# K of an attention decode loaded in 8 KB rows, with successive rows alternating between the partition halves

## The chip, the cores and the metric

The kernel runs on one core of a Trainium2 chip. Inputs lie in HBM; 16 DMA engines copy them to SBUF, where the tensors of this kernel have up to 128 partitions (rows). SP is the engine that issues these loads here; TensorE multiplies matrices, into PSUM; VectorE and ScalarE work on elements. A packet is one entry of the trace's record of DMA transfers. The metric is the device time of one execution in microseconds (us). Eight executions of the kernel before took 196.13 to 197.31 us, seven of them 196.13 to 196.50. Ratios are the mean time of one kernel's fast runs over that of the other's of the same rounds, so they are not quite the ratios of the medians quoted beside them. A single look ("one run") carries no state; it is used only for differences far larger than the scatter.

## The reference

One decode step of attention with a sliding window: 32 batches, 32 query heads, 8 key/value heads, head size 128, and the last 512 of 2048 cached positions.

```
q = (x @ wq)                                  # x: 32 x 512, wq: 512 x 4096
k, v = k_cache[:, :, -512:, :], v_cache[:, :, -512:, :]   # 32 x 8 x 512 x 128, bf16
p = softmax(q . k * 128**-0.5)                # four query heads share a key head
out = (p . v) @ wo                            # wo: 4096 x 512
```

K and V are read once, 33.6 MB each; wq and wo add 8.4 MB. For each of the 32 batches the core needs 1 MB of K and 1 MB of V. The inputs are so small that the softmax is nearly uniform. "Correct" below therefore says little about K.

## The kernel before

SP issues all loads. A batch of K is two loads of 512 KB (four heads each), a batch of V likewise. Each load fills 128 partitions with one row of 4 KB: partition 4s+g holds 16 consecutive positions (chunk s of 32) of head g.

```
NS = 32; NR = 16
K_sb = sb("K_sb", [P, NK, 2, NR, DH], BF16)

def cache_rows(cache, b, h):
    return cache[b, 4*h:4*h+4, SK-W:, :].rearrange("g (s r) d -> s g (r d)", s=NS)

def load_k(b):
    if b >= NK:
        sp.wait_ge(pe_T[3], b - NK + 1)
    for h in range(2):
        sp.dma_start(K_sb[:, b % NK, h].rearrange("p r d -> p (r d)"),
                     cache_rows(k_cache, b, h)).then_inc(sem_k[b % NK][h], 16)
...                                   # load_v: the same with V_sb and sem_v
for b in range(B + LEAD):             # LEAD = 5: K runs five batches ahead of V
    if b < B: load_k(b)
    if b >= LEAD: load_v(b - LEAD)
```

TensorE transposes K (32 products per batch), VectorE and ScalarE copy the result to KT_sb, TensorE makes the scores of four batches in S_ps, in PSUM, and then come softmax, another transpose, and the products with V. The constant `perm` orders the columns of the transposed K, so the placing of rows on partitions can be chosen freely.

Of the kernel before, what the change touches and what calls it, by code (L numbers as in the profile page):

```python
# [1 line left out]

# [3 lines left out]
BF16 = mybir.dt.bfloat16  # L6
F32 = mybir.dt.float32
ACTF = mybir.ActivationFunctionType
ALU = mybir.AluOpType
# [3 lines left out]
def bass_standalone__sliding_block_cached__sampling_kernel(  # L13
# [16 lines left out]
    G4 = 4  # L30
    NR = 16
    NS = 32
    DKT = D // 128
    SCALE = float(DH) ** -0.5
    P = 128
# [11 lines left out]
    with ExitStack() as es:  # L47
# [4 lines left out]
        w_sb = sb("w_sb", [P, DKT * HD], BF16)  # L52
        wq_sb = w_sb[:, :].rearrange("p (kt n) -> p kt n", kt=DKT)
        wo_sb = w_sb[:, :].rearrange("p (g i n) -> p g i n", g=NHG, i=4)
        K_sb = sb("K_sb", [P, NK, 2, NR, DH], BF16)
        V_sb = sb("V_sb", [P, NV, 2, NR, DH], BF16)
        KT_sb = sb("KT_sb", [P, NKT, 2, NR, G4, NS], BF16)
        QT_sb = sb("QT_sb", [P, HQ, B], BF16)
        QBD = sb("QBD", [P, NQB, G, 32], BF16)
        P_f32 = sb("P_f32", [P, W], F32)  # L60
# [4 lines left out]
        band = sb("band", [P, 4, 224], BF16)  # L65
        xT_sb = sb("xT_sb", [P, DKT, 32], BF16)
        ident = sb("ident", [P, P], BF16)
        perm = sb("perm", [P, G4, NS], BF16)
        x_sb = sb("x_sb", [32, D], BF16)
        out_sb = sb("out_sb", [32, 4, 128], BF16)  # L70
        maxv = sb("maxv", [P, NQUAD], F32)
# [10 lines left out]
        sem_x = sem("sem_x")  # L82
        sem_wq = [sem(f"sem_wq{i}") for i in range(DKT)]
        sem_wo = [sem(f"sem_wo{i}") for i in range(NHG)]
        sem_k = [[sem(f"sem_k{i}_{h}") for h in range(2)] for i in range(NK)]
        sem_v = [sem(f"sem_v{i}") for i in range(NV)]
        sem_out = sem("sem_out")
        pe_xT = sem("pe_xT")
# [26 lines left out]
        pool_init = sem("pool_init")  # L115
        pool_qbd = sem("pool_qbd")
        nc.scalar.dma_start(x_sb[:, :], x.rearrange("b s d -> b (s d)")).then_inc(sem_x, 16)
        nc.sync.dma_start(wq_sb[:, 0, :], wq[0:P, :]).then_inc(sem_wq[0], 16)  # L118
        block = es.enter_context(nc.Block())

        def score_row(h, j):
# [1 line left out]

        def cache_rows(cache, b, h):
            return cache[b, 4 * h:4 * h + 4, SK - W:, :].rearrange("g (s r) d -> s g (r d)", s=NS)

        @block.sync
        def _(sp):
            for kt in range(1, DKT):
                sp.dma_start(wq_sb[:, kt, :], wq[kt * P:(kt + 1) * P, :]).then_inc(sem_wq[kt], 16)  # L130

            def load_k(b):
                if b >= NK:
                    sp.wait_ge(pe_T[3], b - NK + 1)
                for h in range(2):
                    sp.dma_start(  # L136
                        K_sb[:, b % NK, h].rearrange("p r d -> p (r d)"), cache_rows(k_cache, b, h)
                    ).then_inc(sem_k[b % NK][h], 16)

            def load_v(b):  # L140
                if b >= NV:
                    sp.wait_ge(pe_PV, b - NV + 1)
                for h in range(2):
                    sp.dma_start(  # L144
                        V_sb[:, b % NV, h].rearrange("p r d -> p (r d)"), cache_rows(v_cache, b, h)
                    ).then_inc(sem_v[b % NV], 16)

            for b in range(B + LEAD):
                if b < B:
                    load_k(b)  # L150
                if b >= LEAD:
                    load_v(b - LEAD)
            sp.wait_ge(pe_qt, 1)
            for hg in range(NHG):
                sp.dma_start(  # L155
                    wo_sb[:, hg].rearrange("p i n -> p (i n)"),
                    wo[hg * 512:(hg + 1) * 512, :].rearrange("(m i) n -> m (i n)", i=4),
                ).then_inc(sem_wo[hg], 16)
            sp.wait_ge(dve_out, 2)
            sp.wait_ge(act_out, 2)  # L160
            sp.dma_start(
                out.rearrange("b s n -> b (s n)"), out_sb[:, :, :].rearrange("b c n -> b (c n)")
            ).then_inc(sem_out, 16)
            sp.wait_ge(sem_out, 16)

        @block.gpsimd
        def _(pool):
            pool.memset(ident[:, :], 0.0).then_inc(pool_init, 1)
            pool.wait_ge(pool_init, 1)
            pool.affine_select(  # L170
                out=ident[:, :], in_=ident[:, :], compare_op=ALU.not_equal, fill=1.0,
                base=0, pattern=[[-1, P]], channel_multiplier=1,
            ).then_inc(pool_init, 1)
            pool.memset(perm[:, :, :], 0.0).then_inc(pool_perm, 1)
            pool.wait_ge(pool_perm, 1)
            pool.affine_select(
                out=perm[:, :, :], in_=perm[:, :, :], compare_op=ALU.not_equal, fill=1.0,
                base=0, pattern=[[-1, G4], [-G4, NS]], channel_multiplier=1,
            ).then_inc(pool_perm, 1)
            pool.memset(junk[:, :], 0.0).then_inc(pool_init, 1)  # L180
            pool.memset(QBD[:, :, :, :], 0.0).then_inc(pool_init, 1)
            pool.memset(P_ex[:, :, :, :], 0.0).then_inc(pool_ex, 1)
            pool.memset(band[:, :, :], 0.0).then_inc(pool_band, 1)
            pool.wait_ge(pool_band, 1)
            pool.affine_select(
                out=band[:, :, :], in_=band[:, :, :], compare_op=ALU.not_equal, fill=1.0,
                base=384, pattern=[[-1, 4], [-4, 224]], channel_multiplier=1,
            ).then_inc(pool_band, 1)
            pool.wait_ge(pool_init, 4)
            pool.wait_ge(dve_qt, 1)  # L190
            pool.wait_ge(act_qt, 1)
            for b in range(B):
                if b >= NQB:
                    pool.wait_ge(pe_S, b - NQB + 1)
                dst = bass.AP(
                    tensor=QBD, offset=(b % NQB) * G * 32 + score_row(0, b % 4),
                    ap=[[NQB * G * 32, P], [G4 * 32 + 16, 2], [32, G4], [1, REP]],
                )
                src = bass.AP(
                    tensor=QT_sb, offset=b,  # L200
                    ap=[[HQ * B, P], [G4 * REP * B, 2], [REP * B, G4], [B, REP]],
                )
                pool.tensor_copy(dst, src).then_inc(pool_qbd, 1)  # L203

        @block.tensor
        def _(pe):
# [23 lines left out]
            def transposes(b):  # L230
                if b == 0:
                    pe.wait_ge(pool_perm, 2)
                for t in range(4):
                    h = t // 2
                    if t % 2 == 0:
                        pe.wait_ge(sem_k[b % NK][h], 16 * (b // NK + 1))
                    if b >= 1:
                        if t < 3:
                            pe.wait_ge(dve_T, 3 * (b - 1) + t + 1)
                        else:  # L240
                            pe.wait_ge(act_T, b)
                    for i in range(8):
                        ins = pe.matmul(  # L243
                            KT_ps[:, t, i * 128:(i + 1) * 128],
                            lhsT=K_sb[:, b % NK, h, 8 * (t % 2) + i, :],
                            rhs=perm[:, :, :],
                            start=True, stop=True, is_transpose=True, tile_position=(0, 0),
                        )
                    ins.then_inc(pe_T[t], 1)

            def scores(b):
                q, j = divmod(b, 4)
                pe.wait_ge(pool_qbd, b + 1)
                pe.wait_ge(dve_T, 3 * b + 3)
                pe.wait_ge(act_T, b + 1)
                if j == 0 and q >= 1:
                    pe.wait_ge(act_exp, q)
                for g in range(G):
                    h, c = divmod(g, G4)
                    ins = pe.matmul(  # L260
                        S_ps[32 * c:32 * c + 32, :],
                        lhsT=QBD[:, b % NQB, g, :],
                        rhs=KT_sb[:, b % NKT, h, :, c, :],
                        start=(j == 0 and h == 0), stop=(j == 3 and h == 1), tile_position=(0, 32 * c),
                    )
                ins.then_inc(pe_S, 1)
# [80 lines left out]
        def _(dve):  # L347
# [9 lines left out]
            def kt_evac(b, t):  # L357
                if t == 0 and b >= NKT:
                    dve.wait_ge(pe_S, b - NKT + 1)
                dve.wait_ge(pe_T[t], b + 1)  # L360
                dve.tensor_copy(  # L361
                    KT_sb[:, b % NKT, t // 2, 8 * (t % 2):8 * (t % 2) + 8, :, :], KT_ps[:, t, :]
                ).then_inc(dve_T, 1)

            def softmax_a(q):
# [7 lines left out]
            def softmax_b(q):  # L373
# [7 lines left out]
                for c in range(G4):  # L381
                    rows = slice(32 * c, 32 * c + 32)
                    dve.tensor_scalar(  # L383
                        P_ex[rows, :, :, c], P_f32[rows, :].rearrange("p (r s) -> p r s", r=NR),
                        recip[rows, q:q + 1], None, op0=ALU.mult,
                    ).then_inc(dve_P, 1)

# [35 lines left out]
        def _(act):  # L423
# [7 lines left out]
            def kt_evac(b):  # L431
                if b >= NKT:
                    act.wait_ge(pe_S, b - NKT + 1)
                act.wait_ge(pe_T[3], b + 1)
                act.activation(  # L435
                    KT_sb[:, b % NKT, 1, 8:16, :, :], KT_ps[:, 3, :], ACTF.Copy
                ).then_inc(act_T, 1)

            def do_exp(q):
# [64 lines left out]
```

## Time and profile before

| | before |
|---|---|
| time, median of 2 runs | 196.62 us |
| DMA rate from 20 to 140 us | 408 GB/s |
| share of the span that TensorE / VectorE are busy | 74% / 52% |
| packet of 4 KB: fastest quarter / mean | 159 / 163 ns |
| packet of 8 KB (wq), median | 309 ns |

Packet times come from the trace's record of every DMA packet; one row is one packet here (17,408 packets of 4 KB and 512 of 8 KB carry K, V, wo and wq).

The following lines of the page before are: the span; the DMA engines' busy share in 40 equal slices of the span, in tenths; what they moved in each slice; and the chain of waits that ended last, by engine.

```profile
span 194.7 us, 6153 instructions
...
DMA  5999999999999999999999999999999999999960
GB/s 204 426 420 406 412 405 411 407 410 407 409 407 407 408 408 410 407 407 410 407 407 410 409 407 407 410 406 408 408 406 411 405 410 405 412 405 412 406 251 31
...
SPq 68%; DMA 23%; PE 5%; issue 3%; DVEq 0%; DVE 0%
```

The engines are busy from the second slice to the 38th at nearly one rate, 405 to 426 GB/s. The chain runs over SP's queue; the reading is that SP issues the next load only as fast as the engines drain earlier ones (issuing one of the K loads took 1.08 us on the median, one of the first wq loads 0.43 us). So DMA is the limit.

The table of stretches of the kernel before has, per row, the stretch, its length, the busy time of five engines (with the number of instructions), the granted TensorE clock, the DMA share and the rate.

```profile
60.00:100.00 40.00, 31.71 (x580) 24.76 (x578) 24.47 (x46) 13.09 (x16) 2.37 (x7) 0.91 1.03 408
100.00:140.00 40.00, 31.33 (x591) 24.80 (x590) 23.22 (x44) 12.65 (x16) 1.79 (x7) 0.91 1.03 408
```

The DMA issues of the page before give the number of loads, the size of each, and the time from issue to landing:

```profile
K_sb<-in_k_cache_dram SPq DMA_DIRECT2D x64, 512.0 KB, 15.6
V_sb<-in_v_cache_dram SPq DMA_DIRECT2D x64, 512.0 KB, 15.4
```

At 15.6 us from issue to landing and 408 GB/s, about twelve loads of 512 KB stand in line, by estimate. The rate above shows no dip between loads (405 to 426 GB/s), so at this depth no cost of a load by itself is to be seen.

### The profile page before, as it was taken

How to read it: one execution, taken by the hardware profiler on the slowest of the kernel's cores; microseconds unless marked ns; L12 is line 12 of the kernel's file. 1: busy time of each engine (PE TensorE's matmuls, PEld its weight loads, DVE VectorE, ACT ScalarE, POOL GpSimd, SP SyncE). 2: the span in 40 equal slices, each digit the busy share in tenths (PEclk: the TensorE clock that was granted, in tenths of full speed). 3: DMA queues.
4: the chain of work that ended last, by engine and by line, in shares of the span. 5: the costliest groups of instructions: out<-in, count | busy, mean ns of one | idle time of the engine just before them, and what ended most of it. 6: DMA issues, size and time to landing. Idle time of an engine off the chain costs nothing.

```text
span 194.7 us, 6153 instructions
## 1 busy us (share of the span) xinstructions
PE 144.0 (74%) x2724; PEld 114.9 (59%) x2724; DVE 102.1 (52%) x190; ACT 57.6 (30%) x70; POOL 15.0 (8%) x45
## 2 busy tenths in 40 slices
PE   0448995877897679749777988779776978937881
PEld 0337773755586567537555667557666667636760
DVE  0005778745684459533944587447943574670211
ACT  3001535622262126213252236204420352213101
POOL 8502000000020001000000000000000000000000
PEclk9999999999699978996999699979998887975558
DMA  5999999999999999999999999999999999999960
GB/s 204 426 420 406 412 405 411 407 410 407 409 407 407 408 408 410 407 407 410 407 407 410 409 407 407 410 406 408 408 406 411 405 410 405 412 405 412 406 251 31
DMA packets 20282, 75.97 MB, mean 390 GB/s; under 512 B 2272, under 2 KB 2336, under 8 KB 19744
## 3 DMA queue, kind: packets, MB, share of 16 engines
q1 hardware_dynamic: 20208, 75.54, 97.2%
q8 instruction: 22, 0.36, 0.8%
q10 hardware_dynamic: 48, 0.03, 0.1%
q14 instruction: 4, 0.03, 0.0%
HBM read 75.53 MB, written 0.03 MB: 388 GB/s over the span
## 4 chain that ended last, share of the span: by engine, by line
SPq 68%; DMA 23%; PE 5%; issue 3%; DVEq 0%; DVE 0%
SPq L144 37%; SPq L136 26%; DMA K_sb<-in_k_cache_dram 15%; DMA w_sb<-in_wo_dram 8%; SPq L155 5%; PE KT_ps L243 4%; SPq L130 1%; PE S_ps L260 1%; PE QO_ps L293 0%; PE KT_ps L337 0%; SPq L118 0%; DVEq L47 0%; DVE out_sb L418 0%
## 5 line engine op out<-in xcount | busy, mean ns | idle before, releaser
L243 PE MATMUL KT_ps<-perm,K_sb 128*128 128x128 bf16 x1024 | 75.2, 235 | 22.4 <-DMA K_sb<-in_k_cache_dram 22.2
L361 DVE COPY KT_sb<-KT_ps 128x1024 bf16<-128x1024 bf16 x96 | 63.6, 689 | 52.2 <-PE KT_ps L243 52.0
L243 PEld LDWEIGHTS KT_ps<-perm,K_sb 128*128 128x128 bf16 x1024 | 65.6, 106 | 30.0 <-DMA K_sb<-in_k_cache_dram 28.4
L435 ACT ACTIVATE KT_sb<-KT_ps 128x1024 bf16<-128x1024 bf16 x32 | 32.8, 1023 | 82.3 <-PE KT_ps L243 82.3
L293 PEld LDWEIGHTS QO_ps<-PT_sb,V_sb 128*128 128x128 bf16 x1024 | 28.3, 97 | 17.8 <-issue 13.5
L293 PE MATMUL QO_ps<-PT_sb,V_sb 128*128 128x16 bf16 x1024 | 31.1, 171 | 3.3 <-DMA V_sb<-in_v_cache_dram 1.3
L383 DVE TENSOR_SCALAR P_ex<-P_f,recip 32x512 bf16<-32x512 f32 x32 | 25.4, 793 | 1.2
L260 PE MATMUL S_ps<-KT_sb,QBD 128*32 128x512 bf16 x256 | 22.2, 428 | 0.0
L453 ACT ACTIVATE PT_sb<-PT_ps 128x1024 bf16<-128x1024 bf16 x16 | 15.5, 1021 | 19.4 <-PE PT_ps L275 19.4
L203 POOL COPY QBD<-QT_sb 128x32 bf16<-128x32 bf16 x32 | 8.5, 279 | 116.1 <-PE S_ps L260 108.1
L275 PE MATMUL PT_ps<-ident,P_ex 128*128 128x128 bf16 x128 | 9.4, 231 | 9.8 <-DVE P_ex L383 9.8
L275 PEld LDWEIGHTS PT_ps<-ident,P_ex 128*128 128x128 bf16 x128 | 7.9, 104 | 10.9 <-DVE P_ex L383 10.8
L397 DVE CAST oT_sb<-QO_ps 128x32 bf16<-128x32 f32 x32 | 9.3, 289 | 7.5 <-PE QO_ps L293 7.5
L221 PE MATMUL PT_ps<-xT_sb,w_sb 128*128 128x32 bf16 x128 | 4.1, 188 | 6.4 <-DMA w_sb<-in_wq_dram 6.4
L367 DVE TENSOR_REDUCE maxv<-S_ps 128x1 f32<-128x512 f32 x8 | 5.5, 691 | 5.4 <-PE S_ps L260 5.4
L221 PEld LDWEIGHTS PT_ps<-xT_sb,w_sb 128*128 128x128 bf16 x128 | 3.7, 104 | 6.8 <-DMA w_sb<-in_wq_dram 4.6
L443 ACT ACTIVATE P_f<-S_ps,negmax 128x512 f32<-128x512 f32 x8 | 5.5, 687 | 6.3 <-DVE negmax L369 6.3
L260 PEld LDWEIGHTS S_ps<-KT_sb,QBD 128*32 128x32 bf16 x256 | 3.9, 96 | 3.9 <-issue 1.4
L353 DVE CAST QT_sb<-PT_ps 128x512 bf16<-128x512 f32 x1 | 0.7, 691 | 10.3 <-PE PT_ps L221 10.3
L337 PE MATMUL KT_ps<-w_sb,o_sel 128*32 128x128 bf16 x128 | 3.8, 289 | 1.9 <-DMA w_sb<-in_wo_dram 1.5
L337 PEld LDWEIGHTS KT_ps<-w_sb,o_sel 128*32 128x32 bf16 x128 | 2.9, 131 | 2.7 <-DMA w_sb<-in_wo_dram 2.2
L427 ACT ACTIVATE QT_sb<-PT_ps 128x512 bf16<-128x512 f32 x1 | 0.6, 597 | 12.0 <-PE PT_ps L221 12.0
(28 smaller groups left out, 22.4 us busy)
## 6 DMA issues: line engine op xcount, KB each, us to landing
K_sb<-in_k_cache_dram SPq DMA_DIRECT2D x64, 512.0 KB, 15.6
V_sb<-in_v_cache_dram SPq DMA_DIRECT2D x64, 512.0 KB, 15.4
w_sb<-in_wq_dram SPq DMA_DIRECT2D x4, 1024.0 KB, 8.3
w_sb<-in_wo_dram SPq DMA_DIRECT2D x8, 512.0 KB, 15.4
x_sb<-in_x_dram ACTq DMA_DIRECT2D x1, 32.0 KB, 2.9
out_dram<-out_sb SPq DMA_DIRECT2D x1, 32.0 KB, 1.5
```

The lines of the kernel that those rows point to most:

```text
L136: sp.dma_start(K_sb[:, b % NK, h].rearrange("p r d -> p (r d)"), cache_rows(k_cache, b, h)).then_inc(sem_k[b % NK][h], 16)
L144: sp.dma_start(V_sb[:, b % NV, h].rearrange("p r d -> p (r d)"), cache_rows(v_cache, b, h)).then_inc(sem_v[b % NV], 16)
L155: sp.dma_start(wo_sb[:, hg].rearrange("p i n -> p (i n)"), wo[hg * 512:(hg + 1) * 512, :].rearrange("(m i) n -> m (i n)", i=4),).then_inc( ...
L243: ins = pe.matmul(KT_ps[:, t, i * 128:(i + 1) * 128], lhsT=K_sb[:, b % NK, h, 8 * (t % 2) + i, :], rhs=perm[:, :, :], start=True, stop=Tru ...
L260: ins = pe.matmul(S_ps[32 * c:32 * c + 32, :], lhsT=QBD[:, b % NQB, g, :], rhs=KT_sb[:, b % NKT, h, :, c, :], start=(j == 0 and h == 0), s ...
L275: ins = pe.matmul(PT_ps[:, r // 8, (r % 8) * 128:(r % 8 + 1) * 128], lhsT=P_ex[:, r, :, :].rearrange("p s g -> p (s g)"), rhs=ident[:, :], ...
L293: ins = pe.matmul(QO_ps[:, 16 * h:16 * h + 16], lhsT=V_sb[:, b % NV, h, r, :], rhs=PT_sb[:, q % 2, r, :].rearrange("p (c n) -> p c n", c=G ...
L361: dve.tensor_copy(KT_sb[:, b % NKT, t // 2, 8 * (t % 2):8 * (t % 2) + 8, :, :], KT_ps[:, t, :]).then_inc(dve_T, 1)
L383: dve.tensor_scalar(P_ex[rows, :, :, c], P_f32[rows, :].rearrange("p (r s) -> p r s", r=NR), recip[rows, q:q + 1], None, op0=ALU.mult,).th ...
L397: dve.tensor_copy(oT_sb[:, :, b], QO_ps[:, 0:HQ]).then_inc(dve_oT, 1)
L435: act.activation(KT_sb[:, b % NKT, 1, 8:16, :, :], KT_ps[:, 3, :], ACTF.Copy).then_inc(act_T, 1)
L453: act.activation(PT_sb[:, q % 2, 8 * i:8 * i + 8, :].rearrange("p r n -> p (r n)"), PT_ps[:, i, :], ACTF.Copy,).then_inc(act_PT, 1)
```

## The change

The intent: K in rows of 8 KB halves the number of K packets, and two packets of 4 KB take longer (2 x 159 ns) than one of 8 KB (309 ns). A batch's window of one head has just 16 rows of 8 KB, so a 1 MB load has 16 x 8 rows. The author writes row (s, g) to partition 4s + g//2 + 64(g%2) by a load that is given its destination shape separately ("shape register"). The eight rows of one s then go to partitions 4s, 4s+64, 4s+1, 4s+65 and so on.

```diff
-                for h in range(2):
-                    sp.dma_start(
-                        K_sb[:, b % NK, h].rearrange("p r d -> p (r d)"), cache_rows(k_cache, b, h)
-                    ).then_inc(sem_k[b % NK][h], 16)
+                spread_load(
+                    sp, K_sb[:, b % NK].rearrange("p r d -> p (r d)"),
+                    k_cache[b, :, SK - W:, :].rearrange("g (s r) d -> s g (r d)", s=KS),
+                ).then_inc(sem_k[b % NK], 16)
...
+        def spread_load(eng, dst, src):
+            row = dst.ap[0][0]
...
+            ins = copy.replace(dma_form, ..., ins=eng.lower_ap_dma(src), ...
+                bass_dst_dge_shape=((4 * row, 16), (row, 4), (64 * row, 2), (1, KR * DH)), ...)
...
-                base=0, pattern=[[-1, G4], [-G4, NS]], channel_multiplier=1,          # perm
+                base=0, pattern=[[-1, G4], [-64, 2], [-G4, KS]], channel_multiplier=1,
...
-                        rhs=KT_sb[:, b % NKT, h, :, c, :],                            # scores
+                        rhs=KT_sb[:, b % NKT, :, g, :],
...
-                        P_ex[rows, :, :, c], P_f32[rows, :].rearrange("p (r s) -> p r s", r=NR),
+                        P_ex[rows, :, :, c].rearrange("p r (s e) -> p r s e", e=2),
+                        P_f32[rows, :].rearrange("p (e r s) -> p r s e", e=2, r=NR),
```

The order of instructions on every compute engine stays as it was. V is loaded as before.

More of the change, by code (lines that the diff above doesn't have):

```diff
@@ L1 @@
+import copy
 from contextlib import ExitStack
@@ L32, in bass_standalone__sliding_block_cached__sampling_kernel @@
     NS = 32
+    KR = 32
+    KS = 16
     DKT = D // 128
@@ L54, in bass_standalone__sliding_block_cached__sampling_kernel @@
         wo_sb = w_sb[:, :].rearrange("p (g i n) -> p g i n", g=NHG, i=4)
-        K_sb = sb("K_sb", [P, NK, 2, NR, DH], BF16)
+        K_sb = sb("K_sb", [P, NK, KR, DH], BF16)
         V_sb = sb("V_sb", [P, NV, 2, NR, DH], BF16)
-        KT_sb = sb("KT_sb", [P, NKT, 2, NR, G4, NS], BF16)
+        KT_sb = sb("KT_sb", [P, NKT, KR, G, KS], BF16)
         QT_sb = sb("QT_sb", [P, HQ, B], BF16)
@@ L67, in bass_standalone__sliding_block_cached__sampling_kernel @@
         ident = sb("ident", [P, P], BF16)
-        perm = sb("perm", [P, G4, NS], BF16)
+        perm = sb("perm", [P, G4, 2, KS], BF16)
         x_sb = sb("x_sb", [32, D], BF16)
@@ L84, in bass_standalone__sliding_block_cached__sampling_kernel @@
         sem_wo = [sem(f"sem_wo{i}") for i in range(NHG)]
-        sem_k = [[sem(f"sem_k{i}_{h}") for h in range(2)] for i in range(NK)]
+        sem_k = [sem(f"sem_k{i}") for i in range(NK)]
         sem_v = [sem(f"sem_v{i}") for i in range(NV)]
@@ L117, in bass_standalone__sliding_block_cached__sampling_kernel @@
         nc.scalar.dma_start(x_sb[:, :], x.rearrange("b s d -> b (s d)")).then_inc(sem_x, 16)
-        nc.sync.dma_start(wq_sb[:, 0, :], wq[0:P, :]).then_inc(sem_wq[0], 16)
+        first = nc.sync.dma_start(wq_sb[:, 0, :], wq[0:P, :])
+        dma_form = first.ins
+        first.then_inc(sem_wq[0], 16)
         block = es.enter_context(nc.Block())
@@ L125, in cache_rows @@
             return cache[b, 4 * h:4 * h + 4, SK - W:, :].rearrange("g (s r) d -> s g (r d)", s=NS)
+        def spread_load(eng, dst, src):
+            row = dst.ap[0][0]
+            part = 1 << 18
+            ins = copy.replace(
+                dma_form, name=nc.get_next_instruction_name(),
+                ins=eng.lower_ap_dma(src), sync_info=None,
+                outs=[eng.lower_ap_dma(dst)[0].__replace__(ap=[[row, P], [1, 1], [1, KR * DH]])],
+                dst_dge_shape=(64 * part, 2, part, 4, 4 * part, 16, 0, 1),
+                bass_dst_dge_shape=((4 * row, 16), (row, 4), (64 * row, 2), (1, KR * DH)),
+                ant_dge_precooked=False,
+            )
+            return eng.add_instruction(ins)
         @block.sync
@@ L173, in _ @@
             ).then_inc(pool_init, 1)
-            pool.memset(perm[:, :, :], 0.0).then_inc(pool_perm, 1)
+            pool.memset(perm[:, :, :, :], 0.0).then_inc(pool_perm, 1)
             pool.wait_ge(pool_perm, 1)
             pool.affine_select(
-                out=perm[:, :, :], in_=perm[:, :, :], compare_op=ALU.not_equal, fill=1.0,
-                base=0, pattern=[[-1, G4], [-G4, NS]], channel_multiplier=1,
+                out=perm[:, :, :, :], in_=perm[:, :, :, :], compare_op=ALU.not_equal, fill=1.0,
+                base=0, pattern=[[-1, G4], [-64, 2], [-G4, KS]], channel_multiplier=1,
             ).then_inc(pool_perm, 1)
@@ L233, in transposes @@
                 for t in range(4):
-                    h = t // 2
-                    if t % 2 == 0:
-                        pe.wait_ge(sem_k[b % NK][h], 16 * (b // NK + 1))
+                    if t == 0:
+                        pe.wait_ge(sem_k[b % NK], 16 * (b // NK + 1))
                     if b >= 1:
@@ L244, in transposes @@
                             KT_ps[:, t, i * 128:(i + 1) * 128],
-                            lhsT=K_sb[:, b % NK, h, 8 * (t % 2) + i, :],
-                            rhs=perm[:, :, :],
+                            lhsT=K_sb[:, b % NK, 8 * t + i, :],
+                            rhs=perm[:, :, :, :],
                             start=True, stop=True, is_transpose=True, tile_position=(0, 0),
@@ L361, in kt_evac @@
                 dve.tensor_copy(
-                    KT_sb[:, b % NKT, t // 2, 8 * (t % 2):8 * (t % 2) + 8, :, :], KT_ps[:, t, :]
+                    KT_sb[:, b % NKT, 8 * t:8 * t + 8, :, :], KT_ps[:, t, :]
                 ).then_inc(dve_T, 1)
@@ L435, in kt_evac @@
                 act.activation(
-                    KT_sb[:, b % NKT, 1, 8:16, :, :], KT_ps[:, 3, :], ACTF.Copy
+                    KT_sb[:, b % NKT, 24:32, :, :], KT_ps[:, 3, :], ACTF.Copy
                 ).then_inc(act_T, 1)
```

## The prediction

> **What bounds the kernel now.** The DMA engines. Slices show them at "9" from the second to the 38th; the table of stretches gives 407 to 410 GB/s in every stretch from 20 us to 180 us, whatever TensorE is doing. TensorE is 74% busy and waits 22.2 us for K (groups by line); VectorE is 52% busy. The chain of waits is 68% SP's queue, held back by transfers, and 23% DMA. SP waits only 1.2 us for buffers. The time is therefore bytes over DMA rate, plus about 3 us of start and 9 us of tail, where engines run dry unevenly (share 0.81, 0.54, 0.27 from 185 us).
>
> **What the change does.** Bytes stay at 75.5 MB. K's 64 loads of 512 KB in 4 KB rows become 32 of 1 MB in 8 KB rows: 8,192 packets become 4,096; semaphore packets fall by 512. The order of work on the other engines is unchanged; scores read KT in runs of 16 columns instead of 32, and the P_ex write interleaves two halves (793 ns each now), both off the critical path.
>
> **Cost from the trace.** Packet records: a 4 KB packet takes 159 ns (fastest quarter), an 8 KB one (wq) 309 ns (median), a semaphore packet 9 ns. Each DMA gives an engine 8 rows and one semaphore: 8x159+9 = 1281 ns per 512 KB, 8x309+9 = 2481 ns per 1 MB; K landings now come 1280 ns apart, wq's wait ends 2.49 us apart, so both sums hold. One K batch goes from 2562 to 2481 ns: 81 ns, times 32 batches = 2.6 us, all on the critical path. The late engines lag the early ones by up to 5.6 us at the last landings.
>
> **The risk.** [...]Alternating by row is meant to keep collisions short[...]. No trace here shows which; I think mostly harmless.
>
> **Time.** 196.6 - 2.6 = 194.0 us. Range 191.0 to 201.0. Faster by over 2%: 0.24; within 2%: 0.54; slower: 0.22.
>
> **What will show it.** Right: packets fall by about 4,600; 8 KB packets stay at 309 ns; the rate in 20 to 180 us rises to 413-416 GB/s; the tail is unchanged. Port collision: 8 KB packets of K well over 309 ns, DMA share above 1, rate under 408.[...]
>
> **What would make it wrong.** Lasting collisions[...]; deeper queues in bytes making SP wait for V buffers; slower score matmuls (428 ns now) letting TensorE bind.

What was stated of the hardware without a measurement of this case is cut from this text, and with it two possible gains, of up to 2 and up to 3 us. The sum is whole: one K batch 81 ns less, times 32, is 2.6 us, and 196.6 - 2.6 = 194.0 us. The two gains were never in it; they only bear on the low end of the range. By a collision the author meant that two DMA engines hold each other up in writing to SBUF. That was an assumption, not shown by the traces of the kernel before.

## The result, and the profile after

The changed kernel took 247.99 us (median of 2, 246.76 to 249.21; before 196.62). The ratio is 1.262, with a 95% interval of 1.256 to 1.269. The prediction of 194.0 us, range 191 to 201, is wrong by 54 us.

The same lines of the page after:

```profile
span 247.4 us, 6122 instructions
...
DMA  6999999999999999999999999999999999999991
GB/s 252 429 293 276 278 285 321 308 306 309 304 309 303 309 313 302 292 301 305 312 323 314 303 305 302 300 293 288 292 293 291 300 297 300 314 406 407 409 376 58
...
DMA 65%; PE 17%; SPq 11%; DVE 4%; issue 1%; ACT 1%; DVEq 0%; ACTq 0%
```

The busy share is the same row of nines. The rate is what fell: from 408 to about 300 GB/s, from the first K load (third slice) to the last (35th). After that, with only V and wo left, it is 406 again. At the same busy share of 1.02 to 1.03 the engines moved 305 GB/s from 60 to 100 us and 408 from 222 to 236.

Stretches of the kernel after, in the same columns; in the last, K has landed:

```profile
20.00:30.00 10.00, 7.44 (x105) 6.08 (x102) 5.85 (x9) 3.07 (x3) 0.47 (x2) 1.00 1.02 277
60.00:100.00 40.00, 27.87 (x439) 22.36 (x438) 19.05 (x36) 9.64 (x12) 2.33 (x6) 0.75 1.02 305
100.00:140.00 40.00, 27.80 (x460) 23.70 (x457) 17.61 (x33) 10.80 (x12) 1.82 (x6) 0.83 1.02 307
222.00:236.00 14.00, 9.32 (x175) 7.45 (x168) 5.34 (x11) 3.42 (x5) 0.00 (x0) 0.62 1.03 408
```

The issues after:

```profile
V_sb<-in_v_cache_dram SPq DMA_DIRECT2D x64, 512.0 KB, 25.3
...
K_sb<-in_k_cache_dram SPq DMA_DIRECT2D x32, 8.0 KB, 26.5
```

(The page sizes a load by its access pattern and so shows 8 KB for these 1 MB loads.)

TensorE's wait for K in all (us, times, longest), before and after:

```profile
PE KT_ps L243 <- DMA K_sb<-in_k_cache_dram: 22.2, 35, 1.3
```

```profile
PE KT_ps L260 <- DMA K_sb<-in_k_cache_dram: 61.5, 28, 5.3
```

The packet records give the size of the loss. K's 8 KB packets took 452 ns on the mean. In the wq loads of the same run the median was 309 (mean 317), and in wide_private below the mean of K was 315. V's 4 KB packets took 205 ns, against 163 before, although nothing in V's addressing changed. Per engine and batch that is:

| packet time per engine and batch | before | after | difference | times 32 batches |
|---|---|---|---|---|
| K | 16 x 163 + 2 x 9 = 2626 ns | 8 x 452 + 9 = 3625 ns | +999 ns | +32 us |
| V | 16 x 163 + 2 x 9 = 2626 ns | 16 x 205 + 2 x 9 = 3298 ns | +672 ns | +21 us |

The sum, 53 us, is nearly the 51 us by which the time grew (packets overlap by 2 to 3%, as the shares of 1.02 and 1.03 show). Longer packets account for the whole loss. TensorE waits for K as a consequence. SP also waited longer for free buffers, 25.9 us against 1.2, but the engines always had work (share 1.02 or 1.03 in every stretch up to 235 us, before the tail), so that is no cause.

### The profile page after: what moved, and what is told of

The parts are those of the page before. It is cut to its first block, busy times and chain, and to the rows that moved or that the text cites. A ratio compares the mean times of both kernels' runs of the same rounds, so it can differ in the third digit from the quotient of the medians.

```text
span 247.4 us, 6122 instructions
## 1 busy us (share of the span) xinstructions
PE 160.5 (65%) x2724; PEld 134.4 (54%) x2724; DVE 103.4 (42%) x190; ACT 57.7 (23%) x70; POOL 15.5 (6%) x45
## 4 chain that ended last, share of the span: by engine, by line
DMA 65%; PE 17%; SPq 11%; DVE 4%; issue 1%; ACT 1%; DVEq 0%; ACTq 0%
DMA K_sb<-in_k_cache_dram 65%; PE KT_ps L260 7%; SPq L162 7%; SPq L121 4%; PE QO_ps L310 3%; DVE P_ex L400 3%; PE S_ps L277 2%; PE KT_ps L322 1%; PE KT_ps L354 1%; PE PT_ps L292 1%; ACT PT_sb L471 1%; SPq L148 1%; DVE oT_sb L415 0%; ACT P_f L461 0%; DVE maxv L384 0%
## 5 line engine op out<-in xcount | busy, mean ns | idle before, releaser
L260 PE MATMUL KT_ps<-perm,K_sb 128*128 128x128 bf16 x1024 | 89.4, 268 | 61.6 <-DMA K_sb<-in_k_cache_dram 61.5
L260 PEld LDWEIGHTS KT_ps<-perm,K_sb 128*128 128x128 bf16 x1024 | 83.2, 124 | 67.0 <-DMA K_sb<-in_k_cache_dram 62.5
L221 POOL COPY QBD<-QT_sb 128x32 bf16<-128x32 bf16 x32 | 9.0, 295 | 157.1 <-PE S_ps L277 149.1
L292 PE MATMUL PT_ps<-ident,P_ex 128*128 128x128 bf16 x128 | 11.0, 255 | 9.2 <-DVE P_ex L400 9.2
L292 PEld LDWEIGHTS PT_ps<-ident,P_ex 128*128 128x128 bf16 x128 | 9.4, 116 | 10.3 <-DVE P_ex L400 10.2
L322 PE MATMUL KT_ps<-oT_sb,band 128*128 128x224 bf16 (+1 forms) x32 | 3.7, 288 | 0.4 <-DVE oT_sb L415 0.4
L354 PE MATMUL KT_ps<-w_sb,o_sel 128*32 128x128 bf16 x128 | 3.3, 290 | 0.4 <-DVE o_sel L433 0.4
## 6 DMA issues: line engine op xcount, KB each, us to landing
K_sb<-in_k_cache_dram SPq DMA_DIRECT2D x32, 8.0 KB, 26.5
```

The costliest lines, as they stand in the source:

```text
L221: pool.tensor_copy(dst, src).then_inc(pool_qbd, 1)
L260: ins = pe.matmul(KT_ps[:, t, i * 128:(i + 1) * 128], lhsT=K_sb[:, b % NK, 8 * t + i, :], rhs=perm[:, :, :, :], start=True, stop=True, is_ ...
L292: ins = pe.matmul(PT_ps[:, r // 8, (r % 8) * 128:(r % 8 + 1) * 128], lhsT=P_ex[:, r, :, :].rearrange("p s g -> p (s g)"), rhs=ident[:, :], ...
```

## The experiments

**The theory.** The port theory: the author supposed that in the changed order pairs of DMA engines, writing to the two halves of the partitions in turn, hold each other up when they are in step and not when one lags the other. Which engine writes which partition was supposed as well: the trace does not name the engine of a packet, so no run shows it. "Private" stands in the names of runs for an order in which nobody is held up. What the runs can show is how the rate and the packets depend on three things: the partitions written, the order of the rows, and extra rows loaded just before (a "pad"), which should make some engines lag.

For runs of R rows and a lag of x rows, the author's estimate is that equal sharing makes a run take 2R - x row times in place of R, and that the lag stays as it is once it is there. From the plain rate of 423 GB/s (ports2) it gives 212, 282 and 423 GB/s for runs of four at a lag of 0, 2 and 4 rows; ports3 measured 223, 296 and 380.

**The rivals.** (1) The load with its own shape, or its packets, are slow. (2) The reads are: 8 KB rows of eight heads lie 512 KB apart in HBM. (3) Only the partitions matter, not the lag. New kernels could not use the load with its own shape, so the experiments build their orders from ordinary loads.

### Small loads alone (ports)

A kernel of loads alone, nine phases with a wait after each.

```
ALT = (0, 64, 1, 65, 2, 66, 3, 67)                   # first partition of each load
every(first, step): 16 partitions first + step*i, one 8 KB row each
plain; small (32,33,34,35) step 4; small (0,1,2,3) step 4; small ALT step 4;
8 more rows, on partitions 0, 4, ..., 28, then small ALT; small 16 consecutive partitions;
outermost source dimension 16; small (0,1,2,3,64,65,66,67); plain
```

> A kernel of loads alone (wrong result on purpose), nine phases with SP waiting between them; every phase loads 8 KB rows, the 1 MB phases 4 MB each. Port theory[...]: 1 plain 128-partition loads, 8 KB packets 309 ns; 2 sixteen rows on partitions 32+4i, 309 ns; 3 the same on 4i[...] about 618 ns; 4 alternating 4i and 64+4i[...], between 400 and 618 ns; 5 the same[...], near 309 ns; 6 sixteen consecutive partitions[...] about 1200 ns; 7 plain loads with an outermost source dimension of 16, above 450 ns[...]; 8 four lower rows then four upper rows, slower than phase 4; 9 as phase 1. HBM theory (reads of the eight heads, 512 KB apart, collide): phases 2 to 8 all slow alike, 1 and 9 also slower than 309 ns. Shape-register theory: none of the phases is slow, since none uses one.

(For the seventh phase the cut clause held a second figure, 309 ns, for the case that its rows were dealt out to the engines as in the first.)

The plain phases gave 309 ns (median). The load with an outermost dimension of 16 gave 624 ns, and sixteen consecutive partitions 1028 ns. The other five phases told nothing, because issuing bound them all. The line of SP's timeline for the eighth phase (start, time, what) shows 32 loads of 128 KB in 20.1 us, 0.63 us each, or 209 GB/s:

```profile
134.62 20.10 SPq L83 DMA_DIRECT2D T<-in_k_cache_dram  x32
```

The packets of the five phases had medians of 436 to 474 ns, even in the second phase (439 ns; 309 was expected). That was not pursued. So where issuing bound, the packet times did not tell these orders of rows apart.

### The load without a shape of its own (natural)

```diff
-   spread_load(sp, K_sb[:, b % NK]..., k_cache[b, :, SK-W:, :].rearrange("g (s r) d -> s g (r d)", s=16))
+   sp.dma_start(K_sb[:, b % NK]..., k_cache[b, :, SK-W:, :].rearrange("g (s r) d -> s g (r d)", s=16))
```

Partition 8s+g, with `perm` to suit.

> The changed kernel without the shape register: one ordinary 1 MB load per batch, source 16 x 8 rows of 8 KB, partition 8s+g (correct result, only the constant perm differs). Port theory[...] as slow as the changed kernel or slower, 250 to 300 us, K packets 450 to 620 ns.[...] Shape-register theory: 194 us. HBM theory: about 248 us.

(Cut with the mapping is a second outcome, 194 us, for rows dealt out as in the kernel before.)

One run: 314.52 us, K packets 577 ns on the mean, V packets 257. It is slower than the changed kernel (248 us, 452 and 205 ns) and its loads are ordinary ones, so such slowness does not need the load with its own shape. Whether that costs something by itself, the next run tells.

### Eight small loads in the changed order (small_alt)

```diff
+   for g in range(8):                               # in place of the one load
+       sp.dma_start(<16 partitions 4i + g//2 + 64*(g%2)>, <16 rows of head g>).then_inc(sem_k[b % NK], 16)
```

> The changed kernel[...] made of eight ordinary loads of 16 rows per batch instead of one load with a shape register (correct result). Port theory and HBM theory: 245 to 255 us, K packets about 440 ns, as the changed kernel. Shape-register theory: 194 to 200 us, K packets 309 ns (the extra semaphore packets cost 7 x 9 ns x 32 = 2 us).

One run: 251.03 us, K packets 434 ns. The whole time and the mean packet are weaker evidence than they look. Ten loads a batch at 0.63 us are 6.3 us of issuing, close to the 7 us that a batch took; the DMA share was 0.94 to 0.97 in its stretches to 180 us; and in ports packets of such loads took 439 ns where 309 was expected.

The opening is better evidence. The 40 slices of small_alt (6.2 us each):

```profile
DMA  6999979999999999999999999889999999999980
GB/s 249 429 296 283 280 194 311 328 313 331 297 316 320 310 297 302 291 336 303 319 314 315 306 308 330 279 290 277 304 307 306 299 299 295 295 404 407 410 332 13
```

In the third to the fifth slice SP is still ahead and only K is loading; in the sixth the queue runs dry (the rate before it is above the 209 GB/s that issuing allows, from loads in stock). From 20 to 30 us the DMA share was 1.03, the rate 284 GB/s and a K packet took 459 ns on the mean; the changed kernel in the same stretch had 1.02, 277 GB/s and 479 ns. The same order of rows in ordinary loads is nearly as slow, so rival 1 falls but for these 2 to 5%.

### 8 KB rows with an outermost dimension of 32, wrong data (wide_private, wide_timed)

```diff
+   k_cache[b, 0:4, 0:2*W, :].rearrange("g (s r) d -> s g (r d)", s=32)   # four heads, twice the window
```

Everything else is the changed kernel: its perm, its scores, its P_ex write. The source has an outermost dimension of 32, as in the kernel before; in natural it was 16. In both runs row n of the load goes to partition n.

> One ordinary 1 MB load per batch in 8 KB rows, but of four heads at twice the window (32 x 4 rows; wrong result on purpose, same bytes, same work)[...]. Port theory: 193 to 195 us, K packets 309 ns: what the prediction took for granted. HBM theory (8 KB rows 512 KB apart read by 16 engines at once): well above 200 us. Shape-register theory: 193 to 195 us.

> The run wide_private again, timed (8 KB rows[...]; wrong result on purpose). Port theory: ratio to the kernel before 0.983 to 0.990, that is 1.4% less, the 2.6 us that the prediction computed.

One run 194.16 us; timed 193.82 (median of 4) against 196.35. The ratio is 0.987, interval 0.986 to 0.989. K packets took 315 ns, V packets 163. The stretch from 60 to 100 us of wide_private, columns as before (the kernel before: 408, the changed one: 305 GB/s):

```profile
60.00:100.00 40.00, 30.66 (x594) 26.17 (x587) 23.14 (x45) 13.48 (x16) 3.01 (x8) 0.91 1.02 414
```

So 8 KB rows pay what was computed for them, and the changed scores and P_ex write cost no visible time.

### Are the reads to blame? (natural_near, quad_private)

```diff
+   natural_near:  k_cache[b, 0:2].rearrange("h (g s r) d -> s (h g) (r d)", g=4, s=16)   # one contiguous MB
+   quad_private:  k_cache[4q:4q+4, :, <128 positions>].rearrange("q g (s r) d -> (q g) s (r d)", s=4)
```

> As the run natural, but its source rows lie 128 KB apart in one contiguous megabyte instead of 512 KB apart (wrong result on purpose). Port theory: 305 to 325 us, as natural. HBM pitch theory: 194 to 205 us.

> As wide_private, one 1 MB load in 8 KB rows with an outermost source dimension of 32, but the rows are those that are really wanted: four batches and eight heads, four rows of each, so four loads bring four batches (wrong result on purpose: the transposes still take a load for one batch).[...] Port theory: 193 to 195 us, the loading a correct kernel could have. HBM theory: reads of 16 engines 512 KB apart collide, 200 to 300 us.

Contiguous reads with an outermost dimension of 16 took 327.01 us, slightly above the range named; reads of heads 512 KB apart with an outermost dimension of 32 took 193.78 (one run each, wrong data). The distance of the reads does not decide: rival 2 falls. In these four runs (natural, wide_private and these two) the loads with 32 were fast (194.16 and 193.78 us) and the loads with 16 slow (314.52 and 327.01); that the dimension changes which engine gets which rows was the author's inference, not shown. The same stretch of quad_private:

```profile
60.00:100.00 40.00, 30.84 (x576) 25.78 (x574) 23.89 (x46) 12.86 (x16) 1.93 (x7) 0.91 1.02 414
```

### Large loads alone (ports2)

Loads alone again, 512 KB or 1 MB each, so that issuing is ahead.

> Loads alone again (wrong result on purpose), now 512 KB or 1 MB per load so that issuing (0.63 us a load, which bound the small loads of the first port kernel) is not the limit; nine phases, 8 KB rows throughout. Port theory: 1 plain 128 partitions 309 ns and about 415 GB/s; 2 partitions 32 to 95[...] as fast as 1; 3 partitions 0 to 63[...] 618 ns, 210 GB/s; 4 sixteen partitions 32+4i with four rows each, as fast as 1; 5 the same on 4i and 64+4i in turn[...]: 210 to 280 GB/s, packets 480 to 618 ns; 6 as 5[...]: 380 to 415 GB/s, packets near 309 ns; 7 outermost source dimension 16[...]: 210 to 230 GB/s; 8 as 7[...]: 380 to 415 GB/s; 9 as 1.[...] HBM theory: phases 1, 2, 3 and 9, whose source is one contiguous block, all fast, and 4 to 8 all slow.

The first five phases in the table of stretches. Columns: stretch, length, POOL (idle), clock, DMA share, GB/s.

```profile
4.00:20.00 16.00, 0.00 (x0) 1.00 1.01 423
26.00:34.00 8.00, 0.00 (x0) 1.00 1.02 373
40.00:56.00 16.00, 0.00 (x0) 1.00 1.02 209
62.00:70.00 8.00, 0.00 (x0) 1.00 1.01 422
76.00:110.00 34.00, 0.00 (x0) 1.00 1.01 222
```

They are: plain, 423 GB/s; partitions 32 to 95, 373; partitions 0 to 63, 209; sixteen partitions 32+4i with four rows each, 422; 4i and 64+4i in turn, in runs of four rows, 222. The median packets were 309, 309, 634, 309 and 625 ns. The second and third phases read blocks of the same form and differ only in the partitions, so where the rows go matters: 373 against 209 GB/s. Why the second ran at 373 and not at the plain 423 was not looked into.

The seventh phase (outermost 16, no pad) gave 218 and the ninth, plain again, 426. The padded phases (6: as the fifth, after four rows to each of partitions 0, 4, ..., 28, 302 GB/s; 8: as the seventh, after four rows to each of 0, 4, 8, 12 and of 32, 36, ..., 76, 227) fell short of the 380 expected. Loads are issued 0.63 us apart (measured in ports), so by the author's estimate a pad of four rows (4 x 309 ns = 1.24 us) had half run off before the next load came, which leaves a lag of two rows. For the sixth phase the estimate of 2R - x then says 423/1.5 = 282, near the 302. For the eighth it does not fit, so both were repeated.

### The lag, set properly (ports3)

Each phase starts with 2 MB of plain loads, so that SP is ahead and the pads should count in full. The lag below is the number of extra rows that a pad writes to each of its partitions.

```
alternate(rows per run, rows of the pad on partitions 0, 4, ..., 28):
(4,0) (4,2) (4,4) (2,0) (2,1) (2,2);  outermost 16: no pad; 4 rows to each of 0, 4, 8, 12 and of 32, 36, ..., 76;
4 rows to each of 0, 4, ..., 28
```

> Loads alone (wrong result on purpose), 8 MB of K rows in each of nine phases, each begun by 2 MB of plain loads so that issuing is ahead of the engines (in ports2 it was not[...]). [...]a run takes 2R-x row times instead of R. Alternating halves in runs of 4 rows: no lag 210 GB/s, lag 2 rows 280 GB/s, lag 4 rows 400 to 420 GB/s. In runs of 2 rows: no lag 210 GB/s, lag 1 row 280, lag 2 rows 400 to 420. Outermost dimension 16: no lag 215[...].[...]

(Of the last two phases, 400 to 420 and 215 GB/s were expected.)

The nine phases in order, columns as above:

```profile
10.00:40.00 30.00, 0.00 (x0) 1.00 1.02 223
55.00:80.00 25.00, 0.00 (x0) 1.00 1.01 296
92.00:110.00 18.00, 0.00 (x0) 1.00 1.02 380
122.00:150.00 28.00, 0.00 (x0) 1.00 1.02 247
165.00:190.00 25.00, 0.00 (x0) 1.00 1.02 255
206.00:225.00 19.00, 0.00 (x0) 1.00 1.02 329
240.00:270.00 30.00, 0.00 (x0) 1.00 1.02 224
285.00:303.00 18.00, 0.00 (x0) 1.00 1.01 380
318.00:350.00 32.00, 0.00 (x0) 1.00 1.01 226
```

The same rows to the same partitions in the same order run at 223, 296 or 380 GB/s, depending only on the pad before them: none, two rows or four. Rival 3 falls. A lag of half a run is not enough; only a lag of a whole run comes near the plain rate (423 in ports2). With the outermost dimension of 16, the pad on 4 and 12 partitions removes most of the loss (224 to 380) and the pad on 8 partitions does nothing (226); the author had expected just that, but from supposed engines, which the trace does not name. In runs of four the estimate holds within 10% (210, 280 and 400 to 420 were expected). In runs of two rows it holds less well: 247, 255 and 329, where the same was expected. Runs of two rows lose less without a lag (247 against 223) and gain less with a whole run of lag (329 against 380). The changed kernel has runs of one row. The rates without a lag, 223 in runs of four and 247 in runs of two, point towards its 277 GB/s (284 in small_alt) for K alone, but that figure is not derived from them: what lag its engines had is not known.

### The lag in the whole kernel (natural_pad, natural_lag)

```diff
+   pad(0, 4); pad(32, 12)          # 32 KB extra to each of partitions 0..3 and of 32..43, unused V buffers
    for b in range(B + LEAD): ...   # as natural
```

> As the run natural (correct result), with two small extra loads before the first K load[...]. Port theory[...]: the first K batches land at nearly the private rate (400 GB/s or more[...]), and the whole is well below natural's 314 us, 200 to 280 us depending on how long the phase holds. If the phase does not matter: 314 to 318 us.

> As natural_pad, but with the two extra loads shaped as in ports3[...]. Port theory: the first K loads, before V joins, at 370 to 415 GB/s instead of natural's 224[...] the whole lies between: 220 to 290 us. If phase is not what costs time in the whole kernel: 312 to 318 us.

The pads did not run as intended. In natural_lag SP waited 17.5 us for them, and the rate was 142 GB/s from 18 to 25 us; in natural_pad it was 79 GB/s from 14 to 20 us. Why was not settled, and the lags that they left are not known. natural_pad took 307.85 us and natural_lag 312.94 (one run each): the whole gained next to nothing. But one stretch is telling. Below, natural first (K alone, then K and V), then natural_lag (K alone after the pads, then K and V), same columns as in the kernel before:

```profile
18.00:38.00 20.00, 13.38 (x156) 10.86 (x157) 7.92 (x12) 4.10 (x4) 0.70 (x3) 1.00 1.02 226
60.00:100.00 40.00, 23.98 (x328) 20.30 (x327) 14.20 (x26) 6.81 (x8) 0.94 (x4) 0.67 1.02 241
```

```profile
26.00:36.00 10.00, 8.31 (x117) 7.18 (x118) 5.85 (x9) 3.02 (x3) 0.47 (x2) 1.00 1.02 382
60.00:100.00 40.00, 23.89 (x319) 19.77 (x320) 13.13 (x24) 6.81 (x8) 0.93 (x4) 0.68 1.02 233
```

The same K loads went at 226 and at 382 GB/s, and the gain was gone once V had joined: natural_lag ran at 392 GB/s from 30 to 35 us, 301 from 35 to 40 and 231 from 40 to 60.

### K and V together (ports4)

Loads alone: 1 MB of K, then the 1 MB of V of the kernel before, again and again. K is plain; alternating in runs of two rows; outermost 16; the same with four rows of lag, by the pads of ports3's eighth phase; on partitions 0 to 31 only; plain.

> Loads alone (wrong result on purpose): 1 MB of K in 8 KB rows, then the 1 MB of V of the kernel before (plain, 4 KB rows[...]), again and again, six phases. Port theory: 1 and 6 K plain: K 309 to 315, V 160 ns, about 410 GB/s. 2 K on alternating halves in runs of two rows: K 400 to 530 ns and V 180 to 220 ns on the mean, 280 to 320 GB/s. 3 K with outermost dimension 16: K 500 to 620, V slow too. 4 the same with four rows of lag[...]: K faster than in 3 but V slower[...] (in natural_lag the gain was gone as soon as V joined). 5 K on partitions 0 to 31 only[...]: V packets[...] stay at 159 to 161 ns, so at least 45% of V's packets do. Fabric theory: in 5 all of V's packets slow down, fewer than 20% at 159 to 161 ns.

| phase | GB/s | K mean, ns | V mean, ns | V packets of at most 173 ns |
|---|---|---|---|---|
| 1 plain | 417 | 314 | 162 | 100% |
| 2 alternating, runs of 2 | 313 | 480 | 181 | 76% |
| 3 outermost 16 | 277 | 570 | 193 | 67% |
| 4 the same, with pads | 236 | 547 | 284 | 4% |
| 5 partitions 0 to 31 | 249 | 607 | 220 | 67% |
| 6 plain | 417 | 314 | 162 | 100% |

The rates are those of the table of stretches; for the second, third and fourth phase its lines are:

```profile
58.00:105.00 47.00, 0.00 (x0) 1.00 1.02 313
118.00:173.00 55.00, 0.00 (x0) 1.00 1.02 277
186.00:254.00 68.00, 0.00 (x0) 1.00 1.02 236
```

My figure for phase 5 missed. At 159 to 161 ns I had asked for 45% of V's packets, or under 20% for the rival; 27% were there (60% in the undisturbed phase 1, so the window was too narrow to start with). The shape is clearer: 67% of V's packets are undisturbed and 26% take over 270 ns, with hardly any between. A slowness of the whole path (the "fabric theory" above) would slow all. What the slow ones wait for is not shown; that it is K rows written to the same part of SBUF is the author's reading, and only the shape supports it. Phase 4 fits natural_lag: with the pads K's packets are a little shorter (547 against 570 ns), but nearly every V packet (96%) takes more than 173 ns, and the sum is worse (236 against 277 GB/s). Neither form, with the pads or without, suited both.

### A correct kernel on the loads of quad_private (quad, quad_u, quad_tok)

quad_private's loads are the right rows, four batches at a time. quad uses them: the scores of one load are 32 products of 128 columns in place of 8 of 512. By the author's account, the placing of K and its scores were verified off the chip with larger inputs, for which K matters.

```diff
+   for j in range(4):
+       for g in range(8):
+           pe.matmul(S_ps[32*c:32*c+32, 128*u:128*u+128], lhsT=QBD[:, (4*q+j) % NQB, g, :],
+                     rhs=KT_sb[:, b % NKT, :, j, g, :], ...)        # c = g % 4; u = b % 4
    P_ex:  quad 8 operations of 256 columns a quad; quad_u 16 of 128 with smaller write steps;
           quad_tok 4 of 512, KT read column by column 256 bytes apart
```

> A correct kernel on the loads of quad_private: 1 MB of K per load in 8 KB rows, four batches and eight heads with four rows each[...]; the scores of a load are 32 products of 128 columns (four batches, 8 heads, a quarter of the window) instead of 8 of 512, and the P_ex write is 8 operations a quad instead of 4. Port theory: the DMA stays the limit, 193 to 195 us, ratio to before 0.983 to 0.992, K packets 309 to 316 ns. If the four times as many score products (TensorE now 73% busy, or reading KT in runs of four columns) or the finer P_ex writes bind: above 196 us with the DMA share falling below 1.

> quad with the P_ex write in 16 operations of 128 columns a quad, each writing 8 byte steps, instead of 8 of 256 in 16 byte steps (894 ns each there). If the P_ex write was what bound quad: operations of 280 to 350 ns, 16 of them about 5 us instead of 7.2 a quad, and the time falls by 5 us or more, to 194 to 201 us. If the four times as many score products bind: 205 to 208 us, as quad.

> quad with the scores' columns in the order of tokens (KT read column by column, 256 bytes apart) and P_ex written by 4 operations of 512 a quad, as before. If the P_ex write was what bound quad: 793 to 800 ns each, 3.2 us a quad, 193 to 197 us. If TensorE reads columns 256 bytes apart more slowly, the score products take well over the 26 us that they took in quad, and the time stays above 200 us.

| kernel | time, us | ratio to before (95%) |
|---|---|---|
| quad | 206.88 | 1.053 (1.048 to 1.057) |
| quad_u | 197.87 | 1.006 (1.002 to 1.011) |
| quad_tok | 213.60 | 1.088 (1.086 to 1.091) |

All three loaded at 413 or 414 GB/s in each stretch from 20 to 140 us, as fast as quad_private; so what they lost, they lost on the compute engines. The line of the P_ex write before, in quad and in quad_u, from the costliest groups (line, engine, operation, shapes, count | busy us, mean ns of one | idle before):

```profile
L383 DVE TENSOR_SCALAR P_ex<-P_f,recip 32x512 bf16<-32x512 f32 x32 | 25.4, 793 | 1.2
```

```profile
L388 DVE TENSOR_SCALAR P_ex<-P_f,recip 32x256 bf16<-32x256 f32 x64 | 44.2, 894 | 1.2
```

```profile
L388 DVE TENSOR_SCALAR P_ex<-P_f,recip 32x128 bf16<-32x128 f32 x128 | 31.0, 363 | 1.2
```

And the scores in quad, then in quad_tok:

```profile
L263 PE MATMUL S_ps<-KT_sb,QBD 128*32 128x128 bf16 x1024 | 26.3, 244 | 7.1 <-issue 6.7
```

```profile
L263 PE MATMUL S_ps<-KT_sb,QBD 128*32 128x128 bf16 x1024 | 79.0, 472 | 0.0
```

The P_ex write was most of what held quad back: half the columns took longer (894 ns) than all of them before (793). The finer form gave 9 us back, of 13 above quad_private, though its operations missed the 280 to 350 ns expected. In quad_tok TensorE became the limit (88% busy), and its P_ex write, in the form of before, took 914 ns where 793 to 800 were expected. None of the three beats the kernel before. What still holds quad_u about 4 us above quad_private was not taken further.

## Why the prediction was wrong

- **The limit.** Right: DMA bound before, and after.
- **The saving of 8 KB rows.** Right in size, shown by wide_timed: 2.5 us saved (193.82 against 196.35), 2.6 predicted; K packets of 8 KB took 315 ns against 2 x 163 (wide_private, before). The changed kernel never collected it.
- **The risk.** This step failed: "No trace here shows which; I think mostly harmless." Lasting collisions stood first among what would make the prediction wrong; but their cost was set to nothing, with the range ending 7 us above the estimate. The step that went wrong: the author took it that a lag of half a row, or loads enough in the queue, would leave no loss. In ports3 a lag of half a run still ran at 296 GB/s and one of a whole run at 380 (423 plain in ports2), and with loads queued throughout (26.5 us from issue to landing) the changed kernel stayed near 300 GB/s until its last K load. In its place the runs showed a K batch of 3625 ns per engine where 2481 were predicted (+37 us over 32 batches) and a V batch of 3298 ns where 2626 were kept (+21 us). Together that is 58 us of packet time against the 54 us by which the prediction was off.
- **"Alternating by row is meant to keep collisions short."** Half right. Shorter runs lose less: without a lag, runs of four rows ran at 223 GB/s and runs of two at 247 (ports3), and runs of one opened at 284 (small_alt). But a lag did not mend itself: in ports3 the first six phases held their rates, by the page's slices inside their stretches (220 and 220; 298 and 297; one slice, 383; 247 and 247; 253 and 255; 327 and 329 GB/s); only the eighth rose, from 369 to 397. It is tempting to take the lags in the changed kernel as random: the estimate (2R - x)/R then averages 1.5, near 452/315 = 1.43. The packet records speak against it. From 20 to 30 us, with K alone, eight tenths of the changed kernel's K packets took between 474 and 486 ns; random lags would spread them from 309 to 618 ns by the same estimate. Nearly all packets were in one state, about 1.5 times 309 ns, from the start; why that one stays open.
- **V.** Not foreseen at all: 205 ns against 163. In ports4, V loads that were alike in form took 162 ns on the mean beside plain K loads and 181 to 284 beside the others.
- **The signs named.** 8 KB packets well over 309 ns and a rate under 408 were seen. "DMA share above 1" was no sign: it was 1.03 before and 1.02 after.
- **Scores and P_ex.** Right: harmless in wide_timed.
- **Still open.** Runs of one row were not measured at a set lag, so the 277 GB/s of the changed kernel's opening is reproduced (small_alt, 284) but not derived. The lag was shown to matter with runs of two and four rows, and in natural_lag's opening stretch with lags that are not known. Which engine writes which partitions was never shown.

## What to carry to other kernels

Before regrouping the rows of a DMA-bound load, time the new order in a kernel of loads alone, together with the other loads that will be in flight: here K in other orders ran at 236 to 313 GB/s beside V, where plain loads ran at 417 (ports4). A saving of 1.3% from larger rows is not worth an access pattern whose rate depends on a lag that the program does not control (223, 296 or 380 GB/s in ports3). Read the DMA rate beside the DMA busy share: the changed kernel's engines looked fully busy (1.02) at 305 GB/s as they did (1.03) at 408.
